# A Fourier mixing layer beside a long convolution: a halved last inverse step, joined first steps and larger transfers

## The chip, the cores and the metric

The kernel runs on one core of a Trainium2 chip. The metric is the time of one launch in device microseconds (us), as the median of several runs; beside it stands one execution that the hardware profiler recorded. The core has five engines with a queue each: PE (matrix products; its weight loads are shown as PEld), DVE (vector operations), ACT (scalar engine: copies and functions), POOL and SP (here they issue transfers, DMAs).

## The reference

Two independent results stand side by side in the output, each 2048 x 512 in float32.

```python
# A: Fourier mixing of x (2048 x 512)
a = einsum("bsd,ed->bse", x, dft_hid_re)
b = einsum("bsd,ed->bse", x, dft_hid_im)
y_A = einsum("ts,bse->bte", dft_seq_re, a) - einsum("ts,bse->bte", dft_seq_im, b)

# B: a state-space layer as a long convolution of u (2048 x 512), 128 states for each of 512 channels
dt = exp(log_dt);  A = -exp(log_A_real) + 1j * A_imag;  C = (C_real + 1j * C_imag) * dt
K = 2 * real(sum_n C[d, n] * exp(A[d, n] * dt[d] * l))          # the kernel's taps, l = 0..2047
y_B = irfft(rfft(u, 4096) * rfft(K, 4096))[:2048] + u * D_skip

out = concatenate([y_A, y_B], axis=-1)
```

## The kernel before

Part A is called FNet in the code, part B Ssm. Both share the core, and the program interleaves them instruction by instruction.

**The plan.** The class Plan is a small simulation that runs on the host while the program is built. Each piece of work is a generator that yields what it needs: an event, a semaphore (a free buffer), or an engine with an estimated duration and an urgency (the lower, the earlier). When the plan grants an engine, the generator emits its instructions. The order in which they are emitted is the order of each engine's queue on the chip, and it is fixed. The steps of part B have urgencies near 1 and go first when they are ready; the FNet products have urgency 5 and fill PE in between. A wrong estimate changes no result, but an instruction may then stand in its queue before its data are there.

**FNet.** In line 366 each group of the "s" kind multiplies x with a quarter of the sequence matrices, and the "p" kind multiplies the result with the hidden matrices. To keep float32 accuracy each operand is split in a high part (made on ACT, line 221) and a rest (on DVE, line 225), and three products are added: 1920 products of 128 x 128 with 512 columns in all. A matrix tile is loaded into a raw buffer (RAWS of them, line 334) and split into one of DEPTH pairs hi and lo; the tiles named in SOFTS are split by transfers from POOL instead (lines 315 to 320).

**Ssm.** The channels are cut into 16 chunks of 32 for the tables, 8 pairs of them for the spectra, and 4 quarters (h = 0 to 3) of 128 for the products of spectra. In this order:

- stage1_u (line 890) makes the first step of the Fourier transform of u and stores it in DRAM as xu.
- tables1 and tables2 make, for each chunk, two tables t1 and t2 of powers (DVE, lines 605, 614, 628, 634). taps (line 801) multiplies them on PE to the taps of the convolution's kernel, ks. There are two buffers for t1 and one for t2.
- stage1_k (lines 824 to 846) makes the first step of the transform of ks and stores it as xk (line 856). Two chunks make one call, two calls one quarter.
- For each quarter h and each q = 0 to 3, load_spectrum (line 965) fetches xu and xk into the tile xt; product finishes both transforms on PE (line 992), copies them to SBUF as uk (ACT, line 1006), multiplies the spectra (DVE, lines 1009 to 1022: two products for each half r, then a difference and a sum), makes the first step of the inverse transform (PE, line 1029, with the constants ia) and stores the result as z to the DRAM array zs (lines 1044, 1053).
- When a quarter's four z are stored, inverse fetches them in two halves (zl, line 1073), makes the last step on PE (line 1078, with the constants ib: 128 rows, 64 columns, 128 streamed elements, 32 products a call), copies it (ACT, line 1084) and stores it (line 1087).

**Buffers.** All PE results of part B share two PSUM slots f0 and f1 (banks and give); a step asks for one or two of them, and requests are served in turn. Set 0 of the SBUF buffers serves h = 0 to 2 with one uk, z, zl and xt each. Set 1 has two of each and serves h = 3; its memory is that of the tables, so it exists only when the last tables are used up and the last xk is stored. For h = 3 the spectra lie in the tiles that held x (x_hi and x_lo), four small tiles for each q.

**Joining.** The class Joined lets a first inverse step of line 1029 wait and be emitted by the next taps, directly in front of the taps' own products. It applies to quarters below JOIN, which is 0, so no step is joined. LATE gives the urgency of a quarter's product.

Of the kernel before, what the change touches and what calls it, by code (L numbers as in the profile page):

```python
# [24 lines left out]
def fft_constants():  # L25
# [21 lines left out]
    return [np.ascontiguousarray(a.astype(np.float32)) for a in (f1u, f1k, w2, ia, ib)]  # L47
# [3 lines left out]
STREAM = 5  # L51
GRAIN = 0.05
# [3 lines left out]
LATE = 1, 1, 3, 1  # L56


def HELD():
    return 1  # L60

# [21 lines left out]
class Plan:  # L83
# [12 lines left out]
    def step(self, p, value):  # L96
        self.now = p[0]
        while True:
# [15 lines left out]
            else:  # L114
                if r[0] != p[5]:
                    p[0] += HOP
                elif r[0] == "dve" and len(r) < 4:
                    p[0] += RESULT
# [45 lines left out]
    def run(self):  # L164

        while self.ready:
# [4 lines left out]
            if engine == "pe":  # L171
# [3 lines left out]
                if stream != self.streaming:  # L175
                    dur += 0.11 if stream else 0.09
# [18 lines left out]
class Fnet:  # L195
# [112 lines left out]
    def soft(self, i):  # L308
        return i[0] == "s" and (2 * i[1] + i[2], i[3]) in SOFTS

# [34 lines left out]
    def matmuls(self):  # L345
        nc = self.nc
        for g in self.groups:
            still = (self.x, self.x_ev) if g[0] == "s" else (self.w, self.w_ev)
            items, acc = self.items[g], []
            for batch in [[i] for i in items[:-BATCH]] + [items[-BATCH:]]:  # L350
                for d in range(4):
# [3 lines left out]
                    for i in batch:  # L355
# [4 lines left out]
                        yield "pe", 0.683, None, 6  # L360
# [48 lines left out]
class Joined(Event):  # L409
# [6 lines left out]
    def run(self, got, shared=True):  # L416
        self.got, self.users = got, {k: 1 for k, _ in got}
        if shared:
            self.users[got[0][0]] = 2
        self.fn(got)  # L420
# [7 lines left out]
class Ssm:  # L428


    def __init__(self, tc, ctx, plan, fnet, nd, ldt, dsk, uG, f1u, f1k, w2, ia, ib, out):
        self.tc, self.nc, self.plan, self.fnet = tc, tc.nc, plan, fnet
        self.nd, self.ldt, self.uG, self.out = nd, ldt, uG, out
# [13 lines left out]
        self.kss, self.res, self.xks = Sem(1), Sem(1), Sem(1)  # L447
        self.waiting, self.taps_left, self.pars = [], 16, Sem(1)
# [28 lines left out]
    def banks(self, n):  # L477
# [8 lines left out]
        return got  # L486

# [295 lines left out]
    def taps(self, ks, n, done):  # L783
# [5 lines left out]
        got = yield from self.banks(2 if other else 1)  # L789
        k, p = got[0]  # L790
        yield "pe", 1.97 + (1.05 if other else 0), None, 320 if other else 256
        if other:
            other.run(got)
# [19 lines left out]
        if other:  # L813
            other.leave(k)
        else:
# [3 lines left out]
    def stage1_k(self, ks, n, ev):  # L819
# [7 lines left out]
        yield "pe", 1.11, None, 64  # L827
# [51 lines left out]
    def stage1_u(self, k):  # L879
# [5 lines left out]
        yield "pe", 1.13, None, 32  # L885
# [34 lines left out]
    def quarters(self):  # L920
# [10 lines left out]
        self.plan.spawn(self.products(), 1)  # L931
        for h in range(4):
            self.plan.spawn(self.inverses(h), 1)

    def take(self):
        yield self.xu_ev
        for h in range(3):
            for q in range(4):
                yield self.sets[0].xts
                xt = self.sets[0].pool.tile([128, 2, 4, 2, PART], F32, name="xt")  # L940
                self.xt[h, q] = [[xt[:, r]] for r in range(2)]
                self.plan.set(self.take_ev[h, q])
        for q in range(4):
            self.xt[3, q] = []
            for r in range(2):
                yield self.fnet.x_free[8 + 2 * q + r]
                self.xt[3, q].append(self.fnet.spare(8 + 2 * q + r, [128, 2, 2, PART]))
# [220 lines left out]
```

## Time and profile before

| | |
|---|---|
| median of 3 runs | 582.6 us (582.21 to 583.75) |
| the profiled execution | 582.56 us, its span 580.8 us |
| PE busy | 571.1 us (98%), 6150 products |
| DVE busy | 512.5 us (88%), 911 instructions |
| ACT busy | 371.2 us (64%), 729 instructions |
| granted PE clock | 0.999 |
| transfers | 133.10 MB in the span, 229 GB/s |

The span reaches from the first to the last instruction of the program, and the profiled execution's time takes in what lies around it. Busy time is the union of an engine's instructions; PE's products overlap in its pipeline, so the mean duration of one is longer than the distance from one start to the next, and what a group costs PE is read from the start of the group to the start of what follows. In the chain that ended last, each piece is followed back to what released it or to the instruction before it on its engine.

### The profile page before, as it was taken

The page shows a single profiled execution, that of the slowest core. Times are in us where ns is not written, and L with a number is a line of the kernel's source. Part 1 is how long each engine was busy: PE and PEld are TensorE (multiplying, and loading weights), DVE is VectorE, ACT ScalarE, POOL GpSimd, SP SyncE. Part 2 cuts the span into 40 slices and gives each one's busy share as a digit, 9 for nine tenths or more (in the row PEclk, how much of TensorE's full clock was granted, in tenths as well). Part 3 has the DMA queues.
Part 4 walks back from the last instruction along what each step waited for, and adds up shares of the span by engine and source line. Part 5 has one row for each costly group of instructions (what it writes and reads, how often), then busy time and mean ns, then how long its engine had stood idle before and what let it go on. Part 6 is the DMA issues. An engine that isn't in the chain of part 4 may idle for free.

```text
span 580.8 us, 15376 instructions
## 1 busy us (share of the span) xinstructions
PE 571.1 (98%) x6150; PEld 436.1 (75%) x6150; DVE 512.5 (88%) x911; ACT 371.2 (64%) x729; POOL 40.3 (7%) x60
## 2 busy tenths in 40 slices
PE   8999999999999999999999999999999999999996
PEld 6877777788777777778877777777687777776685
DVE  6999999999999999999999999999989999346410
ACT  4779665763777595768568585945588744445522
POOL 0000000000100000100000001001100000000000
PEclk9999999999999999999999999999999999999999
DMA  8999999986469767876797887479989995789564
GB/s 248 327 372 263 280 294 276 285 262 170 133 159 239 207 171 218 205 180 207 207 222 190 237 216 226 125 186 296 243 280 262 243 282 184 209 251 303 169 195 144
DMA packets 147831, 133.10 MB, mean 229 GB/s; under 512 B 47280, under 2 KB 107312, under 8 KB 147504
## 3 DMA queue, kind: packets, MB, share of 16 engines
q1 hardware_dynamic: 139408, 117.05, 66.7%
q0 software_dynamic: 8064, 14.68, 12.6%
q8 instruction: 48, 0.79, 0.6%
q10 hardware_dynamic: 288, 0.39, 0.2%
q14 instruction: 23, 0.19, 0.1%
HBM read 89.36 MB, written 42.73 MB: 227 GB/s over the span
## 4 chain that ended last, share of the span: by engine, by line
PE 70%; DVE 23%; issue 4%; DMA 2%; SPq 0%; ACT 0%; DVEq 0%; ACTq 0%
PE acc L366 55%; DVE prod L605 8%; DVE t L614 4%; PE f L992 4%; PE f L801 3%; DVE lo L225 3%; PE f L1029 3%; PE f L1078 2%; PE f L890 2%; DVE t L634 1%; PE f L832 1%; DVE z L1009 1%; DVE cs L675 1%; DMA zl<-zs 1%; DVE uk L1011 1%
## 5 line engine op out<-in xcount | busy, mean ns | idle before, releaser
L366 PE MATMUL acc<-hi,x_hi 128*128 128x512 f32 x640 | 258.2, 403 | 0.3 <-ACT hi L221 0.3
L366 PE MATMUL acc<-lo,x_hi 128*128 128x512 f32 x640 | 250.2, 391 | 0.0
L366 PE MATMUL acc<-hi,x_lo 128*128 128x512 f32 x640 | 249.7, 390 | 0.1
L605 DVE TENSOR_TENSOR prod<-t,cs 128x1024 f32<-128x1024 f32 (+4 forms) x192 | 163.1, 867 | 1.7 <-ACT t L723 0.6
L366 PEld LDWEIGHTS acc<-hi,x_hi 128*128 128x128 f32 x640 | 120.1, 188 | 49.8 <-issue 23.7
L366 PEld LDWEIGHTS acc<-hi,x_lo 128*128 128x128 f32 x640 | 120.3, 188 | 26.5 <-DVE x_lo L225 0.5
L366 PEld LDWEIGHTS acc<-lo,x_hi 128*128 128x128 f32 x640 | 120.3, 188 | 23.0 <-DVE lo L225 0.2
L221 ACT ACTIVATE hi<-raw 128x512 fp32r<-128x512 f32 x132 | 82.6, 627 | 64.0 <-PE acc L366 48.5
L225 DVE TENSOR_TENSOR lo<-raw,hi 128x512 fp32r<-128x512 f32 x132 | 90.1, 684 | 28.2 <-ACT hi L221 21.9
L614 DVE TENSOR_TENSOR t<-prod 128x512 f32<-128x512 f32 (+4 forms) x192 | 94.0, 511 | 1.0
L621 ACT ACTIVATE square<-t 128x256 f32<-128x256 f32 (+1 forms) x64 | 36.7, 573 | 31.0 <-DVE t L614 28.3
L320 POOL DMA_DIRECT2D lo<-in_sT x28 | 24.3, 868 | 214.1 <-ACT lo L318 33.8
L1006 ACT ACTIVATE uk<-f 128x1024 f32<-128x1024 f32 x32 | 31.1, 1017 | 11.8 <-PE f L992 11.8
L801 PEld LDWEIGHTS f<-t,t 128*32 128x32 f32 x2048 | 29.5, 110 | 7.9 <-issue 5.8
L801 PE MATMUL f<-t,t 128*32 128x64 f32 x2048 | 32.4, 220 | 1.9 <-issue 1.4
L389 ACT ACTIVATE y<-acc 128x512 f32<-128x512 f32 x47 | 28.0, 595 | 8.7 <-PE acc L366 8.6
L1009 DVE TENSOR_TENSOR z<-uk 128x512 f32<-128x512 f32 x32 | 21.9, 684 | 9.6 <-ACT uk L1006 7.4
L315 POOL DMA_DIRECT2D hi<-in_sT x28 | 16.2, 577 | 189.4 <-PE acc L366 147.0
L1044 ACT ACTIVATE z<-f 128x512 f32<-128x512 f32 x32 | 17.7, 592 | 13.3 <-PE f L1029 13.3
L634 DVE TENSOR_TENSOR t<-square 128x128 f32<-128x128 f32 (+1 forms) x64 | 24.6, 385 | 0.0
L992 PE MATMUL f<-xt,w 64*32 64x256 f32 x768 | 23.5, 379 | 0.0
L1011 DVE TENSOR_TENSOR uk<-uk 128x512 f32<-128x512 f32 x32 | 22.1, 690 | 0.9
(94 smaller groups left out, 490.7 us busy)
## 6 DMA issues: line engine op xcount, KB each, us to landing
raw<-in_sT SPq DMA_DIRECT2D x99, 256.0 KB, 5.4
p<-y SPq DMA_DIRECT2D x32, 256.0 KB, 3.2
xk<-xk_sb SPq DMA_DIRECT2D x32, 256.0 KB, 5.2
zs<-z SPq DMA_DIRECT2D x32, 256.0 KB, 3.3
zl<-zs SPq DMA_DIRECT2D x16, 512.0 KB, 5.0
raw<-p SPq DMA_DIRECT2D x32, 256.0 KB, 4.4
hi<-in_sT POOLq DMA_DIRECT2D x28, 256.0 KB, 4.6
lo<-in_sT POOLq DMA_DIRECT2D x28, 256.0 KB, 4.9
```

The lines of the kernel that those rows point to most:

```text
L221: self.nc.scalar.activation(hi, src, AF.Copy)
L225: self.nc.vector.tensor_tensor(lo, src, hi.bitcast(F32), op=OP.subtract)
L366: nc.tensor.matmul(acc[d], l[:, cols], r, start=k == 0 and n == 0, stop=k == len(items) - 1 and n == 2)
L389: self.nc.scalar.activation(y, ps, AF.Copy, scale=-1.0 if g[2] == 1 else 1.0)
L605: self.nc.vector.tensor_tensor(p.rearrange("p k d c m -> p k (d c) m"), src.rearrange("p d c l -> p (d c) l")[:, None, :, rows].to_broadca ...
L614: self.nc.vector.tensor_tensor(dst[:, :, :, rows], p[:, 0], p[:, 1, :, ::-1], op=OP.add)
L621: self.nc.scalar.activation(sq, t[:, :, :, m // 2:m], AF.Square)
L634: self.nc.vector.tensor_tensor(t[:, :, 0, m:2 * m:2], box[0][:, :, 0], box[0][:, :, 1], op=OP.subtract)
L801: nc.tensor.matmul(ps[32 * j:32 * j + 32, i], t1[:, d, c], t2[:, d, c], start=c == 0, stop=c == 1, tile_position=(0, 32 * j))
L992: nc.tensor.matmul(got[r][1][32 * xx:32 * xx + 32, g, 256 * c:256 * c + 256], self.w2[rows, 2 * q + r, xx, 32 * c:32 * c + 32], xt[rows].r ...
L1006: a.activation(uk[:, r].rearrange("p g c n d -> p g (c n d)"), p, AF.Copy)
L1011: v.tensor_tensor(t[:, r], t[:, r], u[:, r, :, ::-1], op=OP.mult)
```

## The change

It has five parts.

1. For h = 2 and 3 (HALVED = 2) inverse2 takes the place of inverse. It fetches z so that the two halves of the sum over s lie beside each other on 64 partitions, adds and subtracts them on DVE (four operations of 512 elements in zsum and in place), and then needs products of 64 rows and 32 columns, 32 of them, on eight places of the array, with new constants ib2. The constants ia get a second set for the q of the upper half. inverse2 uses buffer set 1 for h = 2 as well; load_ib2 fetches ib2 (512 KB) into set 1. The output is put in order on the host by a transposition.
2. JOIN = 2: the first inverse steps of h = 0 and 1 are emitted in front of a taps group.
3. For h < 3 the two products of both halves are made in one DVE operation each, of 1024 elements, after both copies of ACT (times).
4. load_spectrum and store_z move a whole q (512 KB) with one transfer instead of two. For h = 3 the loads stay four for each q, one for each small tile.
5. Settings: RAWS 5 instead of 7, DEPTH 5 instead of 4, LATE of h = 2 from 3 to 1.5, and some of the plan's estimated durations. SOFTS holds the same 28 tiles as before. WAITS = 0, so no inverse of line 1078 is joined, and the code for it is left out here.

```diff
-    i = np.zeros((32, 2, 2, 32))
-    i[:, 0, 0], i[:, 0, 1], i[:, 1, 0], i[:, 1, 1] = np.cos(chi), np.sin(chi), -np.sin(chi), np.cos(chi)
-    ia = np.tile(i.reshape(32, 2, 64), (4, 1, 1))
+    i = np.zeros((32, 2, 2, 2, 32))
+    for half in range(2):
+        a = chi + half * 2 * np.pi * l2 / 64
+        i[:, half, 0, 0], i[:, half, 0, 1], i[:, half, 1, 0], i[:, half, 1, 1] = np.cos(a), np.sin(a), -np.sin(a), np.cos(a)
+    ia = np.tile(i.reshape(32, 2, 2, 64), (4, 1, 1, 1))
...
+    ib2 = ib[:64].reshape(64, 2, 2, 8, 32, 2).transpose(2, 0, 1, 3, 5, 4).reshape(128, 16, 2, 32)
...
-LATE = 1, 1, 3, 1
+LATE = 1, 1, 1.5, 1
...
 def taps(self, ks, n, done):
         other = self.waiting.pop(0) if self.waiting else None
-        got = yield from self.banks(2 if other else 1)
+        late = self.late.pop(0) if self.late and not other else None
+        got = yield from self.banks(2 if other or late else 1)
...
         if other:
-            other.run(got)
+            self.ia_done()
+        other = other or late
+        if other:
+            other.run(got, users)
...
 def take(self):
-                xt = self.sets[0].pool.tile([128, 2, 4, 2, PART], F32, name="xt")
-                self.xt[h, q] = [[xt[:, r]] for r in range(2)]
+                xt = self.sets[0].pool.tile([128, 8, 2, PART], F32, name="xt")
+                self.xt[h, q] = [xt]
...
 def load_spectrum(self, name, h, q, view):
         yield "dma", load(512, 270), FAST
-        for r in range(2):
-            for p, xt in enumerate(self.xt[h, q][r]):
-                n = xt.shape[1]
-                self.nc.sync.dma_start(xt[:, :, "uk".index(name)], view[2 * q + r, :, n * p:n * p + n])
+        for p, xt in enumerate(self.xt[h, q]):
+            n = xt.shape[1]
+            self.nc.sync.dma_start(xt[:, :, "uk".index(name)], view[q, :, n * p:n * p + n])
...
 def product(self, b, h, q, got, done):
-            yield "dve", dve(512)
-            v.tensor_tensor(P[:, r], t[:, r], u[:, r], op=OP.mult)
-            yield "dve", dve(512), *APART
-            v.tensor_tensor(t[:, r], t[:, r], u[:, r, :, ::-1], op=OP.mult)
+            if h == 3:
+                yield from times(slice(r, r + 1), LAST)
...
+        def times(r, urgency=None):
+            n = 512 * (r.stop - r.start)
+            yield "dve", dve(n), urgency
+            v.tensor_tensor(P[:, r], t[:, r], u[:, r], op=OP.mult)
+            yield "dve", dve(n), urgency, True
+            v.tensor_tensor(t[:, r], t[:, r], u[:, r, :, ::-1], op=OP.mult)
         for r in range(2):
             self.plan.spawn(half(r, *got[r]), LATE[h])
         yield ready
+        if h < 3:
+            yield from times(slice(0, 2))
...
-                        nc.tensor.matmul(got[xx // 2][1][64 * g:64 * g + 64, xx % 2, :2 * PART], self.ia[rows, c],
+                        nc.tensor.matmul(got[xx // 2][1][64 * g:64 * g + 64, xx % 2, :2 * PART], self.ia[rows, q // 2 if h >= HALVED else 0, c],
...
 def store_z(self, h, q, t, sem):
-        for r in range(2):
-            self.nc.sync.dma_start(view[2 * q + r], t[:, r])
+        self.nc.sync.dma_start(view[q], t.rearrange("p r x d -> p (r x) d"))
...
 def inverses(self, h):
         yield self.zs_ev[h]
-        b = self.sets[h // 3]
+        if h >= HALVED:
+            yield self.ib2_ev
+        b = self.sets[int(h >= min(HALVED, 3))]
         for i in range(2):
             yield b.zls
-            self.plan.spawn(self.inverse(b, h, i, 16), 1)
+            self.plan.spawn((self.inverse2 if h >= HALVED else self.inverse)(b, h, i, 16), 1)
+
+    def load_ib2(self):
+        yield self.set_ev[1]
+        yield self.zs_ev[1]
+        self.ib2 = self.sets[1].pool.tile([128, 16, 2, 32], F32, name="ib2")
+        yield "dma", load(512)
+        self.nc.sync.dma_start(self.ib2, self.ib2_in)
+        self.plan.set(self.ib2_ev)
+
+    def inverse2(self, b, h, i, n):
+        nc, c = self.nc, n // 2
+        z = b.pool.tile([128, 2, c, PART], F32, name="zl", bufs=b.n)
+        view = self.zs[h].rearrange("(a s) c l d -> (s c) a l d", a=2)
+        yield "dma", load(64 * n, 270), FAST
+        for y in range(2):
+            o = n * i + c * y
+            nc.sync.dma_start(z[64 * y:64 * y + 64], view[:, :, o:o + c])
+        t = b.pool.tile([128, c, PART], F32, name="zsum", bufs=b.n)
+        for w in range(0, c, 4):
+            m = slice(w, w + 4)
+            yield "dve", dve(512)
+            nc.vector.tensor_tensor(t[:, m], z[:, 0, m], z[:, 1, m], op=OP.add)
+            yield "dve", dve(512), *APART
+            nc.vector.tensor_tensor(z[:, 1, m], z[:, 0, m], z[:, 1, m], op=OP.subtract)
+        (k, ps), = yield from self.banks(1)
+        yield "pe", 1.06, None, 64
+        for o in range(0, c, 2):
+            for x in range(4):
+                for y in range(2):
+                    r, w = slice(64 * y, 64 * y + 64), o + x // 2
+                    nc.tensor.matmul(ps[32 * x:32 * x + 32, y, PART * (o // 2):PART * (o // 2) + PART],
+                                     self.ib2[r, c * i + w, x % 2], (t, z[:, 1])[x % 2][r, w], start=True, stop=True,
+                                     tile_position=(64 * y, 32 * x))
+        for y in range(2):
+            yield "act", act(512)
+            nc.scalar.activation(z[:, 0, 4 * y:4 * y + 4].rearrange("p w d -> p (w d)"), ps[:, y], AF.Copy)
+        self.give(k)
+        yield "dma", load(32 * n, 270)
+        nc.sync.dma_start(self.out[:, c * i:c * i + c, PART * h:PART * h + PART], z[:, 0])
+        self.plan.put(b.zls)
...
-CHUNK, FIRST, JOIN = 32, 128, 0
-RAWS, DEPTH, STAGED, AHEAD = 7, 4, 4, 3
+CHUNK, FIRST, JOIN = 32, 128, 2
+HALVED = 2
+RAWS, DEPTH, STAGED, AHEAD = 5, 5, 4, 3
```

More of the change, by code (lines that the diff above doesn't have):

```diff
@@ L55, with LAST @@
 APART = None, True
-LATE = 1, 1, 3, 1
+LATE = 1, 1, 1.5, 1
 def HELD():
     return 1
+def LAST():
+    return LATE[3]
 def FAST():
@@ L414, in __init__, with run @@
         self.ssm, self.fn, self.got = ssm, run, None
[L416 to L420, printed above, removed]
+    def run(self, got, users, zone=0):
+        self.got, self.users, self.zone = got, users, zone
+        for k, _ in got:
+            users[k] = users.get(k, 0) + 1
+        self.fn(got, zone)
     def leave(self, k):
@@ L447, in __init__ @@
         self.kss, self.res, self.xks = Sem(1), Sem(1), Sem(1)
+        self.late, self.ia_left = [], 16
         self.waiting, self.taps_left, self.pars = [], 16, Sem(1)
@@ L486, in banks, with ia_done @@
         return got
+    def ia_done(self):
+        self.ia_left -= 1
+        while len(self.late) > self.ia_left:
+            self.plan.set(self.late.pop(0))
     def give(self, k):
```

109 lines of the change are left out of this document (71 added, 38 removed).

## The prediction

> **What bounds the kernel now.** I read the page first, then what PE waited for, then the stretches, and last the chain at the end.
>
> ```profile
> span 580.8 us, 15376 instructions
> ...
> PE 571.1 (98%) x6150; PEld 436.1 (75%) x6150; DVE 512.5 (88%) x911; ACT 371.2 (64%) x729; POOL 40.3 (7%) x60
> ...
> DVE  6999999999999999999999999999989999346410
> ```
>
> PE is busy in 571.1 of 580.8 us, so what shortens the kernel has to shorten PE's own list of work, or at least not hold it up. DVE stands at nine tenths in all but two of the first 34 of 40 slices and falls to a third or two after that. The profiled execution took 582.56 us, 1.76 us more than its span; the median of the three timed runs is 582.6 us, so I add 1.8 us to a span and compare with 582.6.
>
> ```profile
> PE acc L241 <- DVE y L238: 1.6, 1, 1.6
> PE f L801 <- issue: 1.4, 1, 1.4
> ...
> PE acc L366 <- ACT hi L221: 0.3, 1, 0.3
> ```
>
> ```profile
> 410.00:500.00 90.00, 90.00 (x1099) 69.20 (x1098) 82.74 (x147) 59.85 (x118) 2.29 (x3) 1.00 0.85 243
> 500.00:560.00 60.00, 60.00 (x635) 44.40 (x635) 27.47 (x42) 28.48 (x45) 0.00 (x0) 1.00 0.78 230
> ```
>
> The first is the list of PE's waits, the first two and the last of five rows, none over 1.6 us. The second gives, for two stretches, busy us of PE, PEld, DVE, ACT and POOL, then clock, DMA share and GB/s: PE has no idle time, at full clock, and DVE is down to 27.47 of 60 us once the tables are done. The FNet matmuls of line 366 are a filler that stands wherever the state-space part is not ready. So there are two bounds: the sum of PE's work, and the chain of the state-space part, which has to end before the filler runs out. The chain's end is this:
>
> ```profile
> 508.82 1.90 PE f L1078 x32
> ...
> 538.32 1.90 PE f L1078 x32
> ...
> 542.48 1.89 PE f L992 x64
> ...
> 550.68 1.05 PE f L1029 x32
> 551.73 15.19 PE acc L366 x66
> 566.92 1.90 PE f L1078 x32
> 568.82 1.58 PE acc L366 x6
> 570.40 1.90 PE f L1078 x32
> 572.29 3.64 PE acc L366 x15
> ```
>
> After the last first step (line 1029) come 15.19 us of filler, two inverses with 1.58 us between them, 3.64 us of filler; PE ends at 575.93 and 4.9 us later the span is over.
>
> ```profile
> L1073 SPq DMA_DIRECT2D zl<-zs x4: 333/428/430, 556.2 to 557.5; - x4
> ...
> DMA to landing us min/median/max: 3.2/4.5/6.8
> ```
>
> This is the view of zl from 556 us on. The last load left at 557.5 and took at most 6.8 us: the data of the last inverse lay there at 564.3, while PE came to it at 570.40. So 6.1 us of the chain are spare, and the filler hides them.
>
> **The change, PE's side.** Four of eight inverses (h = 2 and 3) become 32 products of 64 rows, 32 columns and 128 streamed elements on eight places of the array. Line 992 uses the same eight places with 256 elements: 64 in 1.89 us, 29.5 ns each; half the elements make 14.8 ns, 32 make 0.47 us. Line 1029 shows the fixed part: 32 of 256 elements on eight places take 1.05 us, 0.11 more than 32 x 29.5 ns. So I take 0.6 us. The ends are 0.47 us (streaming alone) and 1.05 us (no gain from the shorter stream). From 1.90 us that saves 1.3 x 4 = 5.2 us, between 3.4 and 5.7. What bears on the issue rate is this:
>
> ```profile
> 429.87 1.99 PE L801 MATMUL f<-t,t 128*32 128x64 f32 x128
> ...
> 431.79 1.97 PE L1078 MATMUL f<-zl,ib 128*64 128x128 f32 x32
> ```
>
> Here 128 small products go from start to the next group in 1.92 us, 15.0 ns each, with a weight load for every one, so 14.8 ns is about what PE can issue. The Trainium skill (TensorE: Matmul & The Clock Gate, "Wait — 56ns, not 53.3ns?") says that start-to-start never drops below about 25 ns however small the product; by it the four would take at least 0.8 us each and save some 4.0 to 4.4 us instead of 5.2. The row above is below that floor, so I go by the row.
>
> Eight first steps (h = 0 and 1) go in front of a taps group, so the FNet stream is left eight times less. One leaving costs:
>
> ```profile
> 248.44 0.39 PE L366 MATMUL acc<-lo,x_hi 128*128 128x512 f32 x1
> 248.67 0.39 PE L366 MATMUL acc<-hi,x_lo 128*128 128x512 f32 x1
> 248.99 1.99 PE L801 MATMUL f<-t,t 128*32 128x64 f32 x128
> 250.91 0.50 PE L366 MATMUL acc<-hi,x_hi 128*128 128x512 f32 x1
> 251.25 0.40 PE L366 MATMUL acc<-lo,x_hi 128*128 128x512 f32 x1
> ```
>
> Start to start is 0.23 us inside the stream, 0.32 into the group and 0.34 after it: 0.20 us more, 1.6 us for eight. The pair of groups at 429.87 and 431.79 shows 1.92 us for taps, as here alone (248.99 to 250.91), so passing from one tiled group to another costs nothing on top. The Trainium skill (TensorEngine Tiling (Array Packing), "Key Properties") says that a change of tiling mode drains the array; by it a joined pair still has three changes where there were four, and the saving would be 0.4 us instead of 1.6. The row speaks against it.
>
> ```profile
> 180.00:375.00 195.00, 11.29 (x256) 5.35 (x256) 1.00 0.76 205
> 375.00:560.00 185.00, 8.95 (x256) 4.72 (x256) 1.00 0.82 236
> ```
>
> These are the stretches with the first and the last eight first steps of line 1029: the first eight take 2.3 us more for the same products, because the second product's operand is still being made by DVE when PE begins. A joined step begins with the next taps, later, and finds it ready. I count 2.0 us of it (0 to 2.3). In all PE loses 5.2 + 1.6 + 2.0 = 8.8 us (3.4 to 9.6): PE's work alone would end at 567.1 and the span at 572.0.
>
> **The change, DVE's and the chain's side.**
>
> ```profile
> L605 DVE TENSOR_TENSOR prod<-t,cs 128x1024 f32<-128x1024 f32 x96 | 116.6, 1218 | 0.7
> ...
> L1009 DVE TENSOR_TENSOR z<-uk 128x512 f32<-128x512 f32 x32 | 21.9, 684 | 9.6 <-ACT uk L1006 7.4 <-DMA x_lo<-xk 2.2
> ```
>
> Twelve products (h < 3) lose two instructions each: 2 x 0.684 - 1.218 = 0.15 us for a pair, 24 pairs, 3.6 us, all before or around the end of the tables, where DVE has no room. The new sums and differences of the inverses are 4 x 4 x 0.684 = 10.9 us, all after the tables, where DVE stands still for half of the time. Only the last inverse's four, 2.7 us, lie on the chain.
>
> ```profile
> 487.48 0.68 DVE L614 TENSOR_TENSOR t<-prod 128x512 f32<-128x512 f32 x1
> ...
> 492.66 0.17 DVE L824 TENSOR_TENSOR ks<-dskip,ks 128x16 f32<-128x16 f32 x1
> ```
>
> After the last table (488.2) the small addition of line 824 stands in DVE's queue behind the last product of h = 2, until 492.66. With that product more urgent (LATE 1.5, not 3) it comes ahead of the last table: what it takes there it gives back here. So the chain's last part starts earlier by about the 3.6 us; I take 3.0 (0 to 5).
>
> Against this, both inverses of h = 2 move behind the last kernel chunk, because their buffers and ib2 exist only then; before, one had run at 508.82, ahead of the last four products. All share two PSUM slots. One inverse's turn is 542.48 - 538.32 = 4.2 us in the chain above. The new one holds a slot for less PE time, but DVE comes before it; I take 2 us for the additional turn, 0 to 4.2, and as much as 5.5 us more if all eight DVE operations of both (8 x 0.684) fall ahead of the last products.
>
> The zl loads now fill 64 partitions each, two in turn. The landing lines of line 912 (64 partitions, 256 KB) and of line 1053 (128 partitions, 256 KB):
>
> ```profile
> DMA to landing us min/median/max: 3.1/4.6/6.3
> ```
>
> ```profile
> DMA to landing us min/median/max: 2.3/3.3/6.1
> ```
>
> The quickest differ by 0.8 us for 256 KB, 1.6 us for 512 KB; four in a row are late by 0 (the halves overlap) to 6.4 us (one by one). I take 1 us, as both halves are in flight together. The Trainium skill (SBUF — State Buffer, "Can I just issue two DMAs to hit both halves?") says that two such transfers serialize; no run here shows such a load.
>
> The chain: 564.3 - 3.0 + 2 + 1 = 564.3 for the last data, 2.7 for DVE, 0.6 for PE, 4.9 to the end: 572.5. Both bounds lie within 1 us, so PE will stand still here and there before the last inverses, since its order is fixed and filler is no longer plentiful. I add 1.7 us for this and for hand-overs, the length of some seven FNet matmuls (0.23 each). Span 574.2, time 576.0.
>
> At nothing I cost: the 24 loads and 16 stores saved (SP's queue; no row of PE's waits names a DMA), the 512 KB of ib2 (behind the h = 3 loads), the later z stores of h = 0 and 1 (the next product waits for the uk buffer, but the taps that it joins are later still), and 5 raw buffers for 7. The last is covered by this row, where the splits wait 48.5 us for a free hi/lo pair, of which there will be 5 instead of 4:
>
> ```profile
> L221 ACT ACTIVATE hi<-raw 128x512 fp32r<-128x512 f32 x132 | 82.6, 627 | 64.0 <-PE acc L366 48.5 <-issue 8.1 <-ACT z L1044 2.6
> ```
>
> If that cover is gone, PE stands still in FNet for some us at the turn of a group.
>
> **The rivals.** (1) The chain doesn't bind: its 6.1 us of spare time hold and PE's sum decides: span 572.0, 573.8 us. For it: the spare time. Against it: both h = 2 inverses in the last part. (2) The half-partition loads go one by one, 5.4 us more than I took, 576.0 + 5.4 - 1.7 (the stops I added fall into this wait) = 579.7 us. For it: the minima above; against it: both halves are in flight at once. It is what the page of the Trainium skill named above would have. (3) The gain is eaten: taps release the single t2 table 1.05 us later in each of eight joined groups, and DVE stands still for most of these 8.4 us; 576.0 + 6 = 582.0, no change. Against it: DVE has the next t1, the splits and the products to do meanwhile. (4) Slower, by the PSUM slots: the start of the last part doesn't move (+3.0), the additional turn costs 4.2 instead of 2 (+2.2) and the DVE operations of h = 2 push the last products by 5.5: 576.0 + 10.7 = 586.7, less 1.7 for the stops: 585.0. It decides from the point where the last zl data land after 572.6 us, which with the 2.7, 0.6 and 4.9 us behind them is the old span.
>
> **How the numbers follow.** Forecast 0.43 (its own range 573.5 to 579), (1) 0.17, (2) 0.15, (3) 0.10, (4) 0.15. A measurement of this kernel tells about 0.3% from no change: 580.9 to 584.3 is the same. Faster: 0.43 + 0.17 + two thirds of (2) = 0.70; same: the rest of (2), most of (3), some of (4), 0.13; slower 0.17. The range reaches from PE's sum with the highest saving (567.1 - 0.8 + 4.9 + 1.8 = 573.0) and without the stop of 1.4 us at line 801, 571.6, to the lower part of (4), 584.5.
>
> **What would show it.** Right: the groups of the new inverse at 0.5 to 0.7 us from start to next start; first steps of h = 0 and 1 directly before taps, and so eight stretches of line 366 fewer; 1024-element products of about 1.22 us; DVE's last table near 488 or earlier and line 832's last group some 3 us earlier; PE idle for the first time, in the last 20 us. Wrong: PE idle of several us before 490, DVE gaps behind joined groups, the last first step well after 551, or the new inverse at over 1 us.

## The result, and the profile after

The changed kernel takes 588.57 us (median of 4 runs, 587.14 to 592.73) against 582.40 us (581.96 to 583.75) of the kernel before on the same chip: a ratio of 1.0112, 95% interval 1.0088 to 1.0135. It is slower by 6.2 us where 576.0 us was forecast, and above the forecast's range, which ended at 584.5. A few executions among all the runs, 663 to 1122 us long, are left out of the medians and ratios as slow ones. The profiled execution took 588.42 us, its span 586.6 us. In the changed kernel's code the lines named before stand at: FNet's products 374 (366 before), taps 820 (801), products of spectra 1012 (992), first inverse step 1056 (1029), old last step 1158 (1078), and new are zsum 1122, zl's difference 1124 and the halved last step 1131.

The page of the changed kernel, with the busy times, the row of VectorE (DVE) over the 40 slices, that of PE's clock, and the queue that brings instructions:

```profile
span 586.6 us, 15572 instructions
...
PE 569.1 (97%) x6278; PEld 435.0 (74%) x6278; DVE 523.0 (89%) x903; ACT 371.2 (63%) x729; POOL 40.5 (7%) x60
...
DVE  6999999999999999999999998899998998746723
...
PEclk9999999999999999999999998999999999999998
...
q8 instruction: 49, 0.80, 0.6%
```

PE's busy time did fall, from 571.1 to 569.1 us, but the span grew by 5.8. So PE stands still more. And DVE, which showed one eight from the second slice to the 34th before, now shows four. The stretches of both kernels say where. Columns: window and its length, busy us of PE, PEld, DVE, ACT, POOL, then clock, DMA share, GB/s. First the kernel before, then the changed one:

```profile
150.00:300.00 150.00, 148.76 (x1789) 115.07 (x1789) 148.66 (x263) 106.68 (x216) 14.25 (x20) 1.00 0.75 199
300.00:400.00 100.00, 99.93 (x1215) 75.98 (x1212) 99.03 (x179) 67.87 (x134) 9.99 (x14) 1.00 0.75 198
```

```profile
150.00:300.00 150.00, 146.46 (x1681) 114.43 (x1683) 146.15 (x251) 104.80 (x211) 15.82 (x22) 1.00 0.69 177
300.00:400.00 100.00, 96.39 (x1234) 74.57 (x1224) 92.58 (x161) 67.12 (x136) 8.59 (x12) 0.98 0.75 209
```

Before, neither engine had slack here: PE was idle 1.31 of 250 us, DVE 2.31. Now PE is idle 7.15 us and DVE 11.27, 9.0 more. The last table, which ended at 488.2 before, ends 11.6 us later (487.48 + 0.68 there, 499.06 + 0.69 here, from the changed kernel's order of time on DVE):

```profile
499.06 0.69 DVE L628 TENSOR_TENSOR t<-prod 128x512 f32<-128x512 f32 x1
```

From there to the end of the span it is 92.6 us before (580.8 - 488.16) and 86.9 after (586.6 - 499.75): behind the tables the change gains 5.7 us. The loss lies wholly ahead of them. The two longest of PE's waits say what kind of loss it is:

```profile
PE f L820 <- issue: 1.8, 1, 1.8
PE f L1012 <- issue: 1.7, 1, 1.7
```

"issue" means that PE waited for nothing that the profile shows: no engine and no transfer is named, and yet the instruction was not running. The chain between 296 and 364 us shows both places (start, us, what):

```profile
298.44 1.05 PE f L1056 x32
299.49 1.92 PE f L820 x128
301.41 2.29 PE acc L374 x9
303.69 1.00 PE f L1012 x26
304.70 1.66 issue
306.36 1.49 PE f L1012 x38
...
352.37 1.11 PE f L1056 x28
353.48 1.58 PE f L820 x101
355.05 1.79 issue
356.84 0.64 PE f L820 x27
```

The first stands in a product that follows a joined group (first step, then taps) after nine FNet matmuls, the second inside a joined group. PE stops in the middle of a group, after 26 of 64 and after 101 of 128 like instructions, where no new operand begins. The number of instructions fits a cause: 6278 products and as many weight loads are 12,556 instructions, and q8 brought 49 blocks of 16 KB, which makes 256 instructions to a block; before, 2 x 6150 instructions came in 48 blocks, again 256 to each. Joined groups pack 320 instructions into 2.97 us. That the blocks come too late was a theory at this point; the run g1 below tests it.

The trace supports it further. It has one packet of q8 from 304.1 to 305.1 us and one from 354.6 to 355.6, and PE goes on 1.3 us after the end of each. The stop of 1.4 us in the kernel before (407.4 to 408.9) ends 1.6 us after such a packet (406.3 to 407.3). The other six joined groups pass without such a stop, so joining alone does not bring one.

The second stop has a sequel. The stretch 358 to 362 us and FNet's rows in it, then a row of DVE:

```profile
358.00:362.00 4.00, 4.00 (x12) 3.14 (x11) 2.29 (x3) 3.99 (x11) 0.45 (x1) 0.57 0.84 194
```

```profile
358.21 0.62 PE L374 MATMUL acc<-hi,x_hi 128*128 128x512 f32 x1
358.62 0.63 PE L374 MATMUL acc<-lo,x_hi 128*128 128x512 f32 x1
359.05 0.63 PE L374 MATMUL acc<-hi,x_lo 128*128 128x512 f32 x1
...
361.61 0.41 PE L374 MATMUL acc<-hi,x_lo 128*128 128x512 f32 x1
```

```profile
362.19 0.85 DVE L619 TENSOR_TENSOR prod<-t,cs 128x128 f32<-128x128 f32 x2 [1.58 <-ACT t L757]
```

Granted clock 0.57 over four microseconds; FNet's matmuls start 0.43 us apart instead of 0.23, from 358.2 to 361.6, 3.4 us: 1.6 us more lost. DVE stands 1.58 us at the end of it, but that is no sequel: in g1 below, without the stop and with the full clock, it stands 1.60 us at the same instruction, because ACT is busy with other work there. The Trainium skill (TensorE: Matmul & The Clock Gate, "Part 1: The HAM clock gate (the "warmup" mystery)") says that PE falls to half clock after an idle window of about 3.4 us and returns after a busy one. The length of the slow stretch agrees (3.4 us); the cause does not as stated, since PE's longest idle time here was 1.79 us, and the stop of 1.66 us at 304.7 was followed by no slow stretch. Nor does the length of the stop alone decide it: at the same place the runs e3 and e4 below stop for 1.75 us each, and from 358 to 362 us the granted clock is 0.60 in e3 and 1.00 in e4. What decides it stays open.

The tail, last: the chain after the last first step, and the view of zl's loads from 555 us on.

```profile
555.81 1.05 PE f L1056 x32
556.86 17.95 PE acc L374 x78
574.81 1.09 PE f L1131 x64
575.89 2.96 PE acc L374 x12
578.86 1.09 PE f L1131 x64
```

```profile
L1117 SPq DMA_DIRECT2D zl<-zs x4: 573/588/598, 563.0 to 565.0; - x4
...
  DMA zl<-zs: 7.0, 2
...
DMA to landing us min/median/max: 3.2/6.1/10.7
```

A halved last step takes 1.09 us, not 0.6. The four loads leave from 563.0 to 565.0 and land at 568.5, 571.0, 573.5 and 575.7, the last 10.7 us after it left: they come one by one, some 2.4 us apart, and DVE stands 7.0 us for them.

### The profile page after: what moved, and what is told of

The parts are those of the page before. It is cut to its first block, busy times and chain, and to the rows that moved or that the text cites. A ratio compares the mean times of both kernels' runs of the same rounds, so it can differ in the third digit from the quotient of the medians.

```text
span 586.6 us, 15572 instructions
## 1 busy us (share of the span) xinstructions
PE 569.1 (97%) x6278; PEld 435.0 (74%) x6278; DVE 523.0 (89%) x903; ACT 371.2 (63%) x729; POOL 40.5 (7%) x60
## 4 chain that ended last, share of the span: by engine, by line
PE 59%; DVE 22%; issue 6%; DMA 6%; ACT 5%; SPq 0%; POOL 0%; DVEq 0%; ACTq 0%; POOLq 0%
PE acc L374 47%; DVE prod L619 7%; DVE t L628 4%; PE f L1012 3%; DVE lo L233 3%; PE f L820 2%; PE f L908 2%; PE f L1056 2%; DMA x_hi<-xu 2%; DMA zs<-z 1%; DVE t L648 1%; DVE t L642 1%; PE f L1158 1%; DMA hi<-in_sT 1%; DMA raw<-p 1%
## 5 line engine op out<-in xcount | busy, mean ns | idle before, releaser
L619 DVE TENSOR_TENSOR prod<-t,cs 128x1024 f32<-128x1024 f32 (+3 forms) x192 | 163.8, 869 | 4.5 <-ACT t L757 2.9
L1037 DVE TENSOR_TENSOR z<-uk 128x1024 f32<-128x1024 f32 (+1 forms) x20 | 20.1, 1006 | 5.6 <-ACT uk L1026 3.3
L694 ACT ACTIVATE cs<-cs 128x352 f32<-128x352 f32 x32 | 15.8, 536 | 13.5 <-DVE cs L689 13.5
```

Of the source, the lines that this page charges most:

```text
L619: self.nc.vector.tensor_tensor(p.rearrange("p k d c m -> p k (d c) m"), src.rearrange("p d c l -> p (d c) l")[:, None, :, rows].to_broadca ...
```

## The experiments

Three causes stood beside each other after the result: the joined groups outrun PE's instructions; the fewer raw buffers or another order of the queues hold things up; the half-partition loads lengthen the tail. Each ratio below is to the kernel before, measured beside the run.

### e1 to e4: one part undone, or one part alone

e1_join0 is the changed kernel with `JOIN = 0`.

> The changed kernel with JOIN = 0, all else as changed. Three theories of the 6.2 us that the change cost: F, joined groups starve PE of instructions (384 of them in 3 us, with more small products close behind), and the stops hold up DVE's tables too; T, the last part is longer, through both halved inverses of h = 2 and through loads that reach only half of the partitions; S, the settings and the DVE order (5 raw buffers, LATE, one wide product) leave DVE idle. F: PE's stops of over 1 us with the cause 'issue' fall from three or more to one, the last table ends 6 to 10 us earlier, 580 to 583 us although eight more leavings of the FNet stream cost 1.6 us. T and S: 588 to 590 us.

Measured: 594.12 us, 1.0186 (1.0167 to 1.0205). Slower still, and above what all three theories expected. Of F's signs half came: PE's stops of over 1 us by "issue" fall from two to one (1.9 us), but the last table ends at 498.4, only 1.4 us earlier. PE's longest wait:

```profile
PE acc L374 <- ACT hi L229: 7.8, 1, 7.8
```

Without joining, the host lays out another order, in which loads of the h = 3 spectra stand ahead of FNet's raw tiles on SP's queue, and PE stops once for 7.8 us. So joining cannot be judged by switching it off: the switch moves all queues.

e2_before_join2 is the kernel before with `JOIN = 2`.

> The kernel before with JOIN = 2 alone. F: eight leavings and waits saved (about 3.5 us) but stops of about 6 us and later tables: 585 to 588 us. T and S: 579 to 582 us, since the joining itself only saves.

Measured: 600.15 us, 1.0313 (1.0270 to 1.0355), above both expectations, with an 8.2 us wait in the tail:

```profile
PE f L1078 <- DMA zl<-zs: 8.2, 1, 8.2
```

The same holds: three of h = 2's products (urgency 3) stand behind the tables, where one did before, and the tail waits for their z. F's stops did not come: with joined groups PE has one stop of over 1 us by "issue", 1.4 us long, as the kernel before.

e3_halved_off is the changed kernel with `HALVED = 4`, all inverses as before.

> The changed kernel with HALVED = 4: every inverse as before, joining and settings as changed (the 512 KB of constants are still loaded). F: PE has 3.2 us more work and the same stops: 589 to 592 us. T: the last part is short again: 582 to 585 us. S: about 590 us.

Measured: 590.22 us, 1.0124 (1.0104 to 1.0144), as F and S expected and T did not; the changed kernel has 1.0112 (1.0088 to 1.0135). The stops near 303 and 355 us stay, so the halved inverse is not the cause. What it gains is too small to be told here; in the profiled executions the time behind the last table is 2.2 us longer without it (89.1 against 86.9).

e4_zl_full keeps the changed kernel's order and loads zl over all 128 partitions:

```diff
-            nc.sync.dma_start(z[64 * y:64 * y + 64], view[:, :, o:o + c])
+            nc.sync.dma_start(z[:, y], wide[:, o:o + c])
```

> The changed kernel, same order of all queues; each zl load of the halved inverse moves the same 512 KB as before but to all 128 partitions, so that the halved inverse works on a wrong arrangement of z (its output for h = 2 and 3 is not the reference's). Loads to half of the partitions run one by one at half the rate if they bind: the last zl data come 5.7 us or less after the first of the four instead of 7.2. T: the last loads land 3.5 to 4.5 us earlier and the kernel is 2 to 4 us faster, 584.5 to 586.5. F and S: PE has little idle time in the last part, so at most 1 us, 587.5 to 588.6.

Measured: 586.68 us, 1.0056 (1.0039 to 1.0074), between the two expectations. The view of zl's loads from 555 us on:

```profile
  DMA zl<-zs: 2.6, 1
...
DMA to landing us min/median/max: 3.3/5.0/6.6
```

DVE waits 2.6 us instead of 7.0; the four loads land 1.3 us apart, the last at 569.8. The ratio falls by 0.0056, but not all of it is the loads: the profiled execution behind the last table is only 1.2 us shorter (585.4 - 499.68 = 85.7 against 86.9), and it has the stop at 355 us without the slow stretch behind it. A part of the loss, then, not the main one.

### f1 to f4: the settings

f1_raws7 is the changed kernel, f2_before_raws5 the kernel before, each with the other's buffer settings; f3_join0_raws7 is f1 with `JOIN = 0`; f4_rest_only is the changed kernel with all settings of before (`JOIN = 0`, `HALVED = 4`, `RAWS, DEPTH = 7, 4`, h = 2's urgency 3), which leaves the wide products, the larger transfers and the new estimates of durations.

```diff
-RAWS, DEPTH, STAGED, AHEAD = 5, 5, 4, 3
+RAWS, DEPTH, STAGED, AHEAD = 7, 4, 4, 3
```

> The changed kernel with the old buffers, RAWS 7 and DEPTH 4, joining and halving as changed. Theory R: the 5 raw buffers cost, since with fewer matrix tiles fetched ahead the FNet stream and DVE's splits stop wherever SP's queue is held up (first steps of u before 110 us, the 16 loads of xu for h = 3 around 480 us): R expects 3 to 5 us less, 583.5 to 585.5, and the stops before 180 us as small as before. F (instructions) expects the joined stops of 300 to 360 us to stay and no more than 1.5 us gain, 587 to 589.

> The kernel before with RAWS 5 and DEPTH 5 alone. R: 586 to 592 us, with stops of the FNet stream on ACT's splits between 440 and 500 us. F: 582 to 584 us, no change.

> The changed kernel without joining and with the old buffers: halved inverses, wide products, larger transfers and LATE 1.5 are left. R and F together: 577 to 581 us, faster than before by the 3.2 us of PE work in the halved inverses less what the longer last part takes. T (the last part binds): 583 to 586 us.

> The changed kernel without joining, without halving, with the old buffers and LATE 3: only the wide products, the larger transfers and the plan's new durations are left. 579 to 583 us by R and F (3.6 us less DVE work before the last table, PE's sum unchanged, so little gain); over 585 us if the wide products or the larger transfers are what costs.

Measured: f1 599.72 us, 1.0296 (1.0275 to 1.0317); f2 610.29, 1.0458 (1.0426 to 1.0491); f3 607.25, 1.0420 (1.0392 to 1.0449); f4 607.86, 1.0417 (1.0379 to 1.0455). PE's longest wait in f1, then in f2, then in f4:

```profile
PE f L1131 <- DVE zsum L1122: 15.4, 2, 13.7
```

```profile
PE f L801 <- issue: 6.7, 3, 3.1
```

```profile
PE f L1158 <- DMA zl<-zs: 8.7, 1, 8.7
```

A different place each time: the last inverses, PE's instructions, the loads of z. None of the times lies in a range that R, F or T expected; only f4's "over 585 us" came, and g2 and g3 below do not bear out the reason given for it. Two of the runs say more on the stops. f1 has the joined groups, and no wait of over 0.3 us by "issue"; f2 has none, and three of 1.6 to 3.1 us, each ended 1.3 to 1.6 us after a packet of q8. So joining is not needed for such a stop, and does not always bring one: where the dense groups fall in the order matters. All eight runs so far except e4 change the order of the queues besides what they were meant to change, e3 least of them. The number of raw buffers as such is thereby not tested, and stays open. From here on I kept the order fixed where I could, and tested the order by itself.

### g1 to g4: parts with the order kept, and the order alone

g1_taps_double changes the taps of joined groups only, and leaves out half of each tap's rows; the order stays:

```diff
+                if other:
+                    for j in range(4):
+                        d = 16 * o + 4 * i + j
+                        nc.tensor.matmul(ps[32 * j:32 * j + 32, 2 * (i // 2):2 * (i // 2) + 2], t1[:, d, 0],
+                                         t2[:, d].rearrange("p c l -> p (c l)"), start=True, stop=True,
+                                         tile_position=(0, 32 * j))
+                    continue
                 for c in range(2):
```

> The changed kernel in its own order, but in the eight joined groups the taps (L820) are issued as half as many matmuls of twice the columns: they overwrite each other and leave the second half of each tap's rows out, so the convolution's numbers are not the reference's; columns streamed, order, transfers and all other engines' work stay. Theory F (the changed kernel's stops at 303 and 352 to 361 us, 2.26, 0.80, 2.09 and 1.60 us, come from TensorE's instructions arriving too late in the dense joined groups): these stops shrink by 4 us or more, the last table ends near 494 us instead of 499.7, and the time is 580 to 584 us, a ratio of 0.996 to 1.003. Rival (the stops come from data, or VectorE sets the pace anyway): the stops stay, or go without moving the last table; 586 to 590 us, ratio 1.006 to 1.013.

Measured: 583.61 us, 1.0020 (1.0004 to 1.0035). The changed kernel's 1.0112 falls by 0.0092, some 5.4 us. A line of its page, its stretch 300 to 400, and its chain near the second stop:

```profile
q8 instruction: 45, 0.74, 0.5%
```

```profile
300.00:400.00 100.00, 98.71 (x1044) 75.86 (x1035) 96.52 (x167) 68.72 (x139) 8.57 (x12) 1.00 0.80 221
```

```profile
351.70 1.11 PE f L1063 x28
352.81 1.89 PE f L820 x64
354.70 6.34 PE acc L374 x27
```

A group of 64 products takes 1.89 us, as 128 did (1.92): PE's streaming is the same, and four blocks fewer are fetched (1024 instructions, 256 to a block). Both stops are gone, and so is the slow clock (1.00 in the stretch). DVE idles 3.5 us there instead of 7.4, and the last table ends at 494.99, 4.8 us earlier. Theory F is shown for these stops, at the upper end of what it expected. It also shows that what PE loses there moves the end nearly one for one: the two stops and the slow stretch are 1.66 + 1.79 + 1.6 = 5.05 us, and the span falls by 4.7 (586.6 to 581.9).

The stops are not all, though. Ahead of the last table DVE idles 11.5 us in the kernel before, 22.4 in the changed kernel and 18.1 in g1. What is left, 6.6 us more than before, lies elsewhere: 2.5 us of it between 150 and 300 us, where g1 changes nothing, and 1.9 us directly ahead of the last table, where DVE waits for a matrix tile that ACT splits (2.2 us in the changed kernel).

g2_before_wide makes only the DVE products wide, in the kernel before, with its order kept; g3_before_wide_dma adds the larger transfers.

```diff
+            come[0] += 1
+            m = slice(r, r + 1) if h == 3 else slice(0, 2) if come[0] == 2 else None
             yield "dve", dve(512)
-            v.tensor_tensor(P[:, r], t[:, r], u[:, r], op=OP.mult)
+            if m:
+                v.tensor_tensor(P[:, m], t[:, m], u[:, m], op=OP.mult)
```

> The kernel before with its order of all queues kept and one part of the change: the products of both halves in one VectorE instruction, for quarters 0 to 2. 12 products save 2 x (683 + 690) - (1219 + 1222) = 305 ns each, 3.7 us of VectorE. Theory O (the parts are worth about what they were costed at, and the changed kernel's loss is in the new order of its queues): 578.5 to 582.5 us, ratio 0.993 to 1.000. Rival W (the wide product itself does the harm, since it waits for both halves' evictions and lets go of its buffers later): over 584 us, ratio above 1.003.

> As g2_before_wide, and the spectra's loads and z's stores in half as many transfers, again in the order of the kernel before. Theory O: 578 to 582.5 us, ratio 0.992 to 1.000, not above the wide products alone by more than 1 us. Rival D (the larger transfers hold up the FNet tiles that queue behind them): 2 us or more above the wide products alone, with TensorE waiting for raw tiles.

Measured: g2 582.8 us, 1.0000 (0.9989 to 1.0011); g3 583.9 us, 1.0023 (1.0003 to 1.0043). From g2's page:

```profile
PE 570.7 (98%) x6150; PEld 435.6 (75%) x6150; DVE 510.9 (88%) x887; ACT 371.9 (64%) x729; POOL 40.2 (7%) x60
```

The 24 instructions fewer take 1.6 us off DVE's busy time (512.5 before), not 3.7, and nothing off the time. The 3.7 was counted from durations, and DVE's instructions overlap: operations of 512 elements start 0.60 us after each other where none waits for the other (487.48, 488.08, 488.68 in the kernel before), not 0.68, and one of 1024 takes 1.14 (500.27 to 501.41 in the changed kernel). By this a pair saves 0.06 us, an estimate of 1.4 us for 24 pairs. And a wide product begins only when both halves are evicted: DVE's idle time ahead of the last table grows by the same 1.6 us (11.5 to 13.1). Rival W fails too: the wide products do no harm. The larger transfers add 1.1 us to the median, a little more than theory O allows and below rival D's 2 us; the two intervals overlap, so whether they cost anything is not settled.

g2 also shows where "issue" alone misleads. Its longest wait of that name is 1.6 us at line 992, exactly between the two halves of a product (after 32 of 64 instructions), and the last packet of q8 ended over 12 us before it. Late instructions do not explain that one.

g4_before_costs is the kernel before with other estimates of PE's durations in the host's plan, and no instruction changed:

```diff
-                        yield "pe", 0.683, None, 6
+                        yield "pe", 0.681, None, 6
...
-                    dur += 0.11 if stream else 0.09
+                    dur += 0.14 if stream else 0.11
```

> The kernel before with the same instructions, buffers and transfers, and only the host's estimates of TensorE's durations set as in the changed kernel (0.681 for 0.683 us a batch, 0.14 and 0.11 for 0.11 and 0.09 us for a change of stream, 1.06 and 1.25 for 1.11 and 1.13 us for the forward steps, 1.15 for 1.05 us for a first inverse step), from which the host lays out another order of the queues. Theory O: a new order alone costs 5 to 25 us, ratio 1.009 to 1.043, with no instruction changed. Rival (orders are worth about the same; the parts make the difference): 581 to 585 us, ratio 0.997 to 1.005.

Measured: 587.92 us, 1.0092 (1.0073 to 1.0110). PE's two longest waits (the first is new, the second was 0.6 us):

```profile
PE f L1029 <- DVE uk L1019: 2.4, 3, 1.1
PE f L832 <- DVE ks L824: 2.1, 3, 1.2
```

5.4 us lost with the same work. The two rows hold 3.9 us more waiting than before: an order that sends PE to a step 0.7 to 0.8 us too soon, six times. Theory O is shown, at the lower end of its range.

### h1 to h3: the two costs together, and the groups further apart

h1_taps_zl has the edits of g1 and e4 at once.

> The changed kernel in its own order with the edits of g1_taps_double and e4_zl_full together: the joined groups' taps in half as many matmuls (half of each tap's rows left out), and the halved inverses' loads over 128 partitions, which leaves z in a wrong arrangement. If the two costs are separate, in the middle and in the tail, they add: 588.6 - 5.0 - 1.9 = 581.7 us, ratio 0.996 to 1.001. If the tail is held by something that the earlier tables only bring forward (one cost seen twice), it stays at 583 to 584.5 us, ratio 1.001 to 1.004.

Measured: 583.01 us, 1.0003 (0.9988 to 1.0017). It lies where two separate costs would put it, but only 0.0017 below g1's ratio, with intervals that overlap. Whether the two add up is not settled. With both relieved the changed kernel takes as long as the kernel before.

h2_comes34 and h3_comes40 leave all of the computation in place and raise only the plan's estimate of how late a block of PE's instructions comes, so that it sets dense groups further apart.

```diff
-ASKED, APART_BY, COMES = 2.0, 3.8, 2.4
+ASKED, APART_BY, COMES = 2.0, 3.8, 3.4
```

> The changed kernel with the whole computation; only the host's estimate of the time that a block of TensorE's instructions takes to come is 3.4 instead of 2.4 us. The order stays the same up to the product that stopped at 303 us, which now follows after one batch less or more of FNet matmuls, and differs from there on. Theory F: the stops at 303 and 352 to 361 us (6.8 us) shrink by 3 us or more, and the time is 583 to 586 us if the later order is no worse. Theory O (any new order of the later queues loses as much): 587 to 600 us.

> As h2_comes34 with 4.0 us: the product that stopped at 303 us comes two FNet batches later. Theory F: the stop at 303 us goes (2.26 to under 1 us), those at 352 to 361 us shrink, 582 to 586 us. Theory O: 587 to 600 us.

Measured: h2 585.18 us, 1.0036 (1.0023 to 1.0049); h3 587.6 us, 1.0090 (1.0063 to 1.0117). h2's PE in order of time, at both places:

```profile
304.49 1.06 PE L1012 MATMUL f<-xt,w 64*32 64x256 f32 x23
306.78 1.50 PE L1012 MATMUL f<-xt,w 64*32 64x256 f32 x41 [1.23 <-issue]
...
354.26 1.12 PE L1056 MATMUL f<-uk,ia 32*64 32x256 f32 x32
355.31 1.99 PE L820 MATMUL f<-t,t 128*32 128x64 f32 x128
```

Three FNet matmuls more ahead of the product shorten the first stop from 1.66 to 1.23 us, and the joined group at 354 runs through, with nothing slow behind it: 3.4 us better than the changed kernel by medians, as theory F says. Its last table ends at 493.65, 6.1 us earlier than the changed kernel's; behind it 2.8 us of that are lost again (89.7 against 86.9). h3 has smaller stops still, 0.4 us by "issue", but its median lies in theory O's range, and its executions part: the profiled one took 584.59 us at a mean granted clock of 0.998, three others 587.3 to 589.5 us at 0.994 to 0.995. What lowers the clock in those is not in a trace and stays open. No version beat the kernel before.

## Why the prediction was wrong, step by step

**Where it held.** The first steps of h = 0 and 1 stand directly ahead of taps, and where no instruction is late the pair takes 1.05 and 1.92 us (298.44 and 299.49 above), as costed. The 1024-element products take the 1.22 us that was forecast. The tail came out near the forecast although two of its terms, below, were wrong. From the last group of line 832, which was to come 3.0 us earlier (495.99 - 3.0 = 492.99), to the end of the span 574.2 - 492.99 = 81.2 us were forecast; 586.6 - 503.37 = 83.2 came.

**The halved step, a term mis-sized.** "I take 0.6 us" was too low: it takes 1.09 us, so four save 0.81 x 4 = 3.2 us instead of 5.2. The code's 32 products are 64 rows of PE in the trace ("x64"), as line 992's 32 products are 64. The old step's "32 products a call", too, are rows: its code has 16. I set 32 against a price for one row of the 64; 64 at 14.8 ns and the 0.11 us of line 1029 would have been 1.06 us. By the row it is 17 ns each, so the rate itself was about right. The Trainium skill's floor of about 25 ns (TensorE: Matmul & The Clock Gate, "Wait — 56ns, not 53.3ns?") was rightly set aside: 64 rows at that floor would have taken 1.6 us, an estimate by the page's figure.

**The loads, a value wrongly chosen.** I took 1 us between 0 and 6.4, "as both halves are in flight together". They come one by one: 575.7 for the last, as rival (2) has it. The Trainium skill (SBUF — State Buffer, "Can I just issue two DMAs to hit both halves?") has it so too, and the landings 2.4 us apart agree. In the time, the loads over 128 partitions are worth 0.0056 of the ratio at most (e4), and 1.2 us in the profiled tails.

**The start of the last part, the step that failed.** "The chain's last part starts earlier by about the 3.6 us; I take 3.0 (0 to 5)." The last table ends 11.6 us later, and the last group of line 832 (850 in the changed kernel) starts 7.4 us later. From the chains of both kernels, and from DVE's order of time in the changed one:

```profile
495.99 1.05 PE f L832 x32
```

```profile
503.37 1.12 PE f L850 x32
```

```profile
500.27 1.22 DVE L1037 TENSOR_TENSOR z<-uk 128x1024 f32<-128x1024 f32 x1
...
503.14 0.17 DVE L842 TENSOR_TENSOR ks<-dskip,ks 128x16 f32<-128x16 f32 x1
```

Three things were wrong in this step. The products' 3.6 us on DVE were mis-sized and then eaten by their later start (g2: 1.6 us off DVE's work, no gain). The last product of h = 2 did not move ahead of the last table: it begins at 500.27, and the small addition (842, before 824) still stands behind it, at 503.14. And, the largest, the work ahead of the tables was priced as if nothing could stop PE there. The profile before had shown such a stop once, as 1.4 us of "issue" at line 801; I used that row only to shift the lower end of the range. Joining puts 320 instructions where 256 stood, and the change as a whole leads to two such stops and a slow stretch in the place of one stop. In a stretch where DVE is idle 1% of the time, these reach the last table. g1 shows 4.8 us of its 11.6, and 5.4 us of the time.

**A silent assumption.** I costed the settings at nothing, with a row for the raw buffers alone. The plan turns every estimate into another order of all queues, and g4 shows such a change to be worth 5.4 us with no instruction changed. How much of the changed kernel's loss is its order apart from the stops is open: with the stops and the loads relieved (h1) 7 us of the forecast gain are still missing, of which 2.0 are the halved step's and up to 3.0 the products' ("I take 3.0"). The rest has no run of its own.

**The rivals.** (4) had the sign and nearly the time (585.0), but not the mechanism: the last table, where its PSUM slots begin to matter, was late already, and what follows it got shorter (92.6 to 86.9 us). (3), DVE standing still behind joined groups, saw the right engine; but with taps releasing t2 at the same moment, g1 brings more than half of DVE's idle time in 300 to 400 us back, so the later release is not the main cause of it.

## What to carry to other kernels

A program of many small products has a second price per product, its place in the instruction stream: look for waits called "issue" in the middle of a group, and for a packet of the instruction queue just ahead of their end, before packing more groups together. In a stretch where two engines are both busy 98% of the time and more, a stop of one can cost nearly its full length at the end (g1), and work taken off one of them alone may gain nothing (g2). Where a planner fixes the order, hold the order while testing a part, and change the order alone to see what it is worth.

## What the runs showed of the hardware that was not expected

- PE's instructions arrive during the run, in blocks of 16 KB and 256 instructions (49 blocks for 12,556; 45 for 11,532). Dense stretches can outrun them: stops of 1.2 to 1.8 us in the changed kernel, e3, e4 and h2, up to 3.1 us in f2. PE went on 1.2 to 1.6 us after the block's packet had ended.
- After a stop of 1.79 us (changed kernel) and one of 1.75 us (e3) PE ran at about half clock for some 3.4 us; after one of 1.75 us (e4) and one of 1.66 us it did not.
- Halving the number of taps' products at twice the columns leaves the group's time as it was (1.89 us for 64, 1.92 for 128). What the fewer instructions gained came from the stops, not from inside the group.
